# A few subtractions and the last combination of an attention chunk move from GpSimd to VectorE, and the attention steps are placed anew

## The chip, the cores and the metric

The kernel runs on one core of a Trainium2 chip. The metric is the device time of one launch in microseconds. The engines are TensorE (PE in the rows, with its weight loads as PEld), VectorE (DVE), ScalarE (ACT), GpSimd (POOL) and the queue of SyncE (SP), which issues the transfers.

## The reference

Causal attention with a recalled memory term feeds a feed-forward layer with a squared ReLU, and that feeds four experts whose outputs are weighted per token.

```python
# q, k, v: (2, 8, 576, 64); M_prev: (2, 8, 64, 64); z_prev: (2, 8, 64)
a = softmax(where(causal, -1e9, q @ k.T / sqrt(64)))          # per batch and head
q_p = where(q > 0, q, exp(q) - 1) + 1
mem = (q_p @ M_prev) / (q_p . z_prev + 1e-6)
g = 1 / (1 + exp(-beta))                                      # per head
x = g * mem + (1 - g) * (a @ v)                               # -> 1152 tokens x 512

h = maximum(x @ w_in, 0) ** 2                                 # w_in: 512 x 2048
x = h @ w_out                                                 # w_out: 2048 x 512

p = domain_probs / (domain_probs.sum(-1) + 1e-9)              # 1152 x 4
out = sum_e p[:, e] * (maximum(x @ w1[e], 0) @ w2[e])         # w1: 4 x 512 x 1024
```

All inputs are float32.

## The kernel before

The 1152 tokens are nine tiles of 128, cut into three chunks that are worked in this order: tiles 7 and 8, tiles 0 to 3, tiles 4 to 6. While one chunk goes through the feed-forward layer, the attention of the next one is computed, so that TensorE has work of two kinds to alternate between. The change lies in the second of these stages: `ffn1(1, ...)`, the feed-forward layer of tiles 0 to 3 (512 tokens), runs beside `attention_b`, the attention of tiles 4 to 6. In the trace it lies between about 119.5 and 262 us.

Precision is kept by splitting each operand into a high and a low part and multiplying three of the four pairs (`PASS`). ScalarE makes the high part by a copy with rounding, another engine the low part by a subtraction. In the rows these are `w` (feed-forward weights, lines 83 and 84), `g` (hidden values, lines 793 and 794), `kst` (keys, lines 543 and 545), `qh` (queries, lines 549 and 550), `vct` (values, lines 566 and 568), `ah` and `al` (attention weights, lines 625 and 626) and `x` (the feed-forward layer's input, lines 205 and 206).

The feed-forward generator runs over 16 blocks f of 128 hidden columns. `up(f)` is 12 matmuls into one PSUM bank, `hpb` (line 106; `hpc` is the same in the stage after), which ScalarE (787) and VectorE (788) turn into `r`. That bank has one buffer, so the next `hpb` waits until `r` on VectorE has read it (the block f = 1 has a bank of its own). `down(f)` is 12 matmuls into the accumulators `y` (804). The generator yields after every three matmuls, 16 x 4 + 16 x 4 times, and once at its start: 129 yields.

`attention_b` goes over four groups j of two heads and, within each, over the tiles 4, 5 and 6. Tile 6 holds the last 64 tokens of both batches. One unit is one tile and one head group: score matmuls `sc` (589), masked maximum on VectorE (189), exponential on ScalarE (617), the split into `ah` and `al`, two transposing transfers on SyncE into `aht` and `alt` (630), and three units later the `pv` matmuls (656), which ScalarE copies to `xl` (661). The `pm` matmuls (669) give the memory term `xm`. Each piece is a step of the generator, and there are 58 of them. Beside the steps, `load(j)` brings in and splits the keys, queries and values of the next head group. The keys are stacked twice over the partitions, and the low part is written into the upper 64 partitions, in two halves for each of two batches: for batch 0 by GpSimd, for batch 1 by VectorE (545).

After the last unit of a tile, `combine` weighs the two terms: five small VectorE operations on `cf` (215 to 219), then `xm` times its weight (220), `xl` times its weight into `to` (223) and the sum (224). Then TensorE transposes `to` into `tp` (197), and ScalarE and VectorE copy that to `x`. The engines for 223 and 224 are arguments of `combine`. 220 is always on GpSimd.

`mix` sets how the two generators alternate: at each yield of the feed-forward layer it adds a ratio to a number that starts below zero, and runs one attention step for each whole one reached.

TensorE's order is the program's order. On the other engines the order is set by a scheduler ahead of time, and each engine runs its queue strictly in that order.

Of the kernel before, what the change touches and what calls it, by code (L numbers as in the profile page):

```python
# [10 lines left out]
F32 = mybir.dt.float32  # L11
# [11 lines left out]
B, H, S, D = 2, 8, 576, 64  # L23
# [21 lines left out]
def spread(a, b, lag=0.0):  # L45

    n = len(a) + len(b)
    keyed = [((i + 0.5) / len(a), 0, x) for i, x in enumerate(a)] + [(lag + (1 - lag) * (i + 0.5) / len(b), 1, x) for i, x in enumerate(b)]
    return [x for _, _, x in sorted(keyed, key=lambda k: k[:2])] if n else []
# [3 lines left out]
def attention_then_experts(ctx, tc, qa, ka, va, qc, kc, vc, mz, beta, w1, probs, w2, out):  # L53
# [11 lines left out]
    nc = tc.nc  # L65
# [47 lines left out]
    def run(g):  # L113
        for _ in g:
            pass

    def mix(main, side, ratio, due=0.0):

        for _ in main:
            due += ratio  # L120
            while due >= 1.0:
                due -= 1.0
                next(side, None)
        run(side)
# [16 lines left out]
    gp = kvs.enter_context(tc.tile_pool(name="gp", bufs=2))  # L141
# [5 lines left out]
    gate1 = kv.tile([P, H], F32, name="gate1")  # L147
# [20 lines left out]
    gate1v = kv.tile([P, H], F32, name="gate1v")  # L168
# [39 lines left out]
    def combine(t, pool, xl, xm, sm, guard, ps, muls, eng, nm=1, gate1=gate1, to=None):  # L208


        cf = pool.tile([P, 2, H], F32, tag="cf", name="cf", bufs=2)
        to = xl if to is None else to

        def zeroth():
            nc.vector.tensor_scalar_add(cf[:, 0], sm, guard)
            nc.vector.tensor_scalar_add(cf[:, 1], xm[:, :, D], 1e-6)
            nc.vector.reciprocal(out=cf, in_=cf)
            nc.vector.tensor_mul(cf[:, 0], cf[:, 0], gate1)
            nc.vector.tensor_mul(cf[:, 1], cf[:, 1], gate)
            nc.gpsimd.tensor_mul(xm[:, :, 0:D], xm[:, :, 0:D], cf[:, 1, :, None].to_broadcast([P, H, D]))  # L220

        def first():
            muls.tensor_mul(to, xl, cf[:, 0, :, None].to_broadcast([P, H, D]))
            eng.tensor_add(to, to, xm[:, :, 0:D])

        return [zeroth, first, lambda: finish(t, to, ps, nm)]
# [294 lines left out]
    def attention_b(pool, ps):  # L521
# [10 lines left out]
        def load(j):  # L532
            kraw, vraw = [], []
            for b in range(B):
                kraw.append(pool.tile([P, 2, S], F32, tag="kraw", name="kraw", bufs=2))
                nc.sync.dma_start(out=kraw[b], in_=kc[b, j])
            qraw = pool.tile([P, 4, 2, P], F32, tag="qraw", name="qraw", bufs=2)
            nc.sync.dma_start(out=qraw, in_=qc[j])
            for _ in range(4):
                yield  # L540
            for b in range(B):
                k = kst[b, j] = pool.tile([P, 2, S], F32R, tag=f"kst{b}", name="kst", bufs=2)
                nc.scalar.activation(out=k, in_=kraw[b], func=AF.Copy)
                for js in (slice(0, 1), slice(1, 2)):
                    (nc.vector if b else nc.gpsimd).tensor_sub(k[64:128, js], kraw[b][64:128, js], k[64:128, js].bitcast(F32))
                yield
                if b == 0:
                    qh = pool.tile([P, 2, 4, 2, P], F32R, tag="qh", name="qh", bufs=2)
                    tc.keep_in_program_order(nc.scalar.activation(out=qh[:, 0], in_=qraw, func=AF.Copy))
                    nc.vector.tensor_sub(qh[:, 1], qraw, qh[:, 0].bitcast(F32))  # L550
                    qst[j] = [qh]
                    yield
            e = pool.tile([P, 4, 2, P], F32, tag="phi", name="phi")
            nc.scalar.activation(out=e, in_=qraw, func=AF.Relu, scale=-1.0)
            nc.scalar.activation(out=e, in_=e, func=AF.Exp, scale=-1.0)
            nc.vector.scalar_tensor_tensor(out=qraw, in0=qraw, scalar=1.0, in1=e, op0=ALU.add, op1=ALU.max)
            qst[j].append(qraw)
            for b in range(B):
                vraw.append(pool.tile([P, 5, 2, D], F32, tag="vraw", name="vraw", bufs=2))
                nc.sync.dma_start(out=vraw[b].rearrange("p k j d -> p k (j d)"), in_=vc[b, j])  # L560
            yield
            for b in range(B):
                vt = vct[b, j] = pool.tile([P, 2, 5, 2, D + 1], F16, tag=f"vct{b}", name="vct", bufs=2)
                for p in range(2):
                    nc.gpsimd.memset(vt[:, p, :, :, D], 1.0 - p)
                nc.scalar.activation(out=vt[:, 0, :, :, 0:D], in_=vraw[b], func=AF.Copy, scale=vs)
                yield
                nc.vector.scalar_tensor_tensor(
                    out=vt[:, 1, :, :, 0:D], in0=vraw[b], scalar=vs, in1=vt[:, 0, :, :, 0:D], op0=ALU.mult, op1=ALU.subtract
                )  # L570
                yield
# [68 lines left out]
        def values(t, j):  # L640

            xl, xm, mx, nb = st[t]
            hs = slice(2 * j, 2 * j + 2)

            def pv_():
                ath, atl = at.pop((t, j))
                pv = ps.tile([P, 2, D + 1], F32, tag="m", name="pv")
                c = 0
                for b, r0, n in TILES[t]:
                    nk = -(-(r0 + n) // P)  # L650
                    qs = slice(c, c + n)
                    for jj in range(2):
                        todo = [(k, a, p) for k in range(nk) for a, p in ((ath, 0), (ath, 1), (atl, 0))]
                        for i, (k, a, p) in enumerate(todo):
                            kr = min(P, r0 + n - k * P)
                            nc.tensor.matmul(  # L656
                                pv[qs, jj, :], lhsT=a[0:kr, jj, k, qs], rhs=vct[b, j][0:kr, p, k, jj, :],
                                start=(i == 0), stop=(i == len(todo) - 1),
                            )
                    c += n  # L660
                nc.scalar.activation(out=xl[:, hs, :], in_=pv, func=AF.Copy)

            def mem():
                e = qst[j][1]
                pm = ps.tile([P, 2, D + 1], F32, tag="m", name="pm")
                for jj in range(2):
                    c = 0
                    for i, (b, r0, n) in enumerate(TILES[t]):
                        nc.tensor.matmul(
                            pm[c:c + n, jj, :], lhsT=e[0:64, t - LAST + i, jj, c:c + n], rhs=mzt[:, b, 2 * j + jj, :],  # L670
                            start=True, stop=True,
                        )
                        c += n
                nc.scalar.activation(out=xm[:, hs, :], in_=pm, func=AF.Copy)

            return pv_, mem

        units = [(t, j) for j in range(4) for t in tiles]
        lag = 3
        late = {}  # L680
        run(load(0))
        ahead = iter(())
        for i in range(len(units) + lag + 3):
            a, m = [], []
            if i < len(units):
                t, j = units[i]
                if t == tiles[0]:
                    run(ahead)
                    ahead = load(j + 1) if j < 3 else iter(())
                a = scores(t, j)  # L690
                m = [values(t, j)[1]]
            m = late.pop(i, []) + m
            if 0 <= i - lag < len(units):
                t, j = units[i - lag]
                m = [values(t, j)[0]] + m
                if j == 3:
                    xl, xm, mx, nb = st[t]
                    to = pool.tile([P, H, D], F32, tag="to", name="to")
                    fs = combine(
                        t, pool, xl[:, :, 0:D], xm, xl[:, :, D], 1e-9 * 2.0**14, ps, nc.gpsimd, nc.gpsimd, gate1=gate1v, to=to  # L700
                    )
                    m = m + [lambda fs=fs: (fs[0](), fs[1]())]
                    late[i + 1] = [lambda fs=fs: fs[2]()()]
            if a or m:
                for f in spread(a, m) if a and m else a + m:
                    f()
                    next(ahead, None)
                    yield
# [160 lines left out]
    with ExitStack() as cb:  # L869
        bp = cb.enter_context(tc.tile_pool(name="bp", bufs=1))  # L870
        with tc.tile_pool(name="ps_2", bufs=1, space=PSUM) as ps_2:
            mix(ffn1(1, ps_2, gp, 1), attention_b(bp, ps_2), 0.54, -11.0)
    kvs.close()


# [348 lines left out]
```

## Time and profile before

| what | us |
|---|---|
| median of three runs (698.75 to 699.38) | 699.31 |
| the profiled execution | 696.58 |
| its span, first to last instruction | 694.8 |
| TensorE busy in the span | 668.8 (96%) |
| VectorE busy | 516.2 (74%) |
| ScalarE busy | 450.0 (65%) |
| GpSimd busy | 159.7 (23%) |

The mean granted TensorE clock of the profiled execution is 0.998 of full speed, the higher of its two levels (2.4 GHz). Busy time of TensorE is the union of its matmuls, whose ends overlap in the pipeline, so a stretch without idle time can show 100%. The profiled execution is 2.7 us faster than the median of the runs, so differences are taken within its own time.

### The profile page before, as it was taken

How to read it: one execution, taken by the hardware profiler on the slowest of the kernel's cores; microseconds unless marked ns; L12 is line 12 of the kernel's file. 1: busy time of each engine (PE TensorE's matmuls, PEld its weight loads, DVE VectorE, ACT ScalarE, POOL GpSimd, SP SyncE). 2: the span in 40 equal slices, each digit the busy share in tenths (PEclk: the TensorE clock that was granted, in tenths of full speed). 3: DMA queues.
4: the chain of work that ended last, by engine and by line, in shares of the span. 5: the costliest groups of instructions: out<-in, count | busy, mean ns of one | idle time of the engine just before them, and what ended most of it. 6: DMA issues, size and time to landing. Idle time of an engine off the chain costs nothing.

```text
span 694.8 us, 12513 instructions
## 1 busy us (share of the span) xinstructions
PE 668.8 (96%) x4604; PEld 481.0 (69%) x4604; DVE 516.2 (74%) x1028; ACT 450.0 (65%) x862; POOL 159.7 (23%) x211
## 2 busy tenths in 40 slices
PE   7799999999999989999999999999999999999997
PEld 4688878776877869999666666666655555555553
DVE  7989786899786567589697579897765856665753
ACT  6789886888775549968777666555534535354440
POOL 1010010212200062003334424443332242423200
PEclk9999999999999999999999999999999999999999
DMA  9898884889585437864122432333331322000002
GB/s 302 259 386 298 273 277 143 291 234 236 163 162 118 101 93 246 302 191 149 62 90 92 122 104 79 122 118 125 123 121 62 94 90 91 30 1 1 2 1 75
DMA packets 65422, 101.25 MB, mean 146 GB/s; under 512 B 32656, under 2 KB 34704, under 8 KB 65360
## 3 DMA queue, kind: packets, MB, share of 16 engines
q1 hardware_dynamic: 65216, 100.45, 46.5%
q8 instruction: 36, 0.59, 0.3%
q14 instruction: 26, 0.21, 0.1%
q10 hardware_dynamic: 144, 0.00, 0.0%
HBM read 82.87 MB, written 10.75 MB: 135 GB/s over the span
## 4 chain that ended last, share of the span: by engine, by line
PE 65%; DVE 14%; DMA 7%; ACT 6%; issue 4%; POOL 2%; SPq 0%; DVEq 0%; ACTq 0%; POOLq 0%
PE o L1112 21%; PE pe L1015 18%; PE y L804 6%; DMA raw<-in_w 4%; PE y L802 4%; PE hpa L101 3%; PE hpb L106 3%; PE hpc L106 3%; PE pv L656 2%; DVE w L84 2%; PE pv L356 1%; PE sc L589 1%; DVE w L923 1%; PE sc L307 1%; DVE a L189 1%
## 5 line engine op out<-in xcount | busy, mean ns | idle before, releaser
L1112 PE MATMUL o<-w,g 128*128 128x512 f16 x864 | 217.5, 379 | 2.8 <-DVE g L1032 1.4
L1015 PE MATMUL pe<-xs,wu 128*128 128x256 f16 (+1 forms) x1344 | 196.3, 286 | 2.0 <-DVE u L1037 1.5
L1015 PEld LDWEIGHTS <-wu 128*128 128x128 f16 x1344 | 131.0, 98 | 70.3 <-issue 4.2
L1112 PEld LDWEIGHTS <-g 128*128 128x128 f16 x864 | 84.2, 98 | 72.0 <-DVE g L1032 2.6
L1031 ACT ACTIVATE g<-h 128x512 f16<-128x512 f32 (+1 forms) x64 | 43.3, 676 | 101.4 <-DVE h L1037 95.8
L804 PE MATMUL y<-g,w 128*128 128x512 f32 (+1 forms) x384 | 89.3, 369 | 0.0
L981 POOL TENSOR_TENSOR ws<-raw 128x256 f32<-128x256 f32 x32 | 24.3, 760 | 269.4 <-DVE wu L978 180.2
L804 PEld LDWEIGHTS y<-g,w 128*128 128x128 f32 x384 | 67.6, 188 | 7.2
L1032 DVE SCALAR_TENSOR_TENSOR g<-h,g 128x512 f16<-128x512 f32 (+1 forms) x64 | 51.4, 803 | 26.8 <-ACT g L1031 26.6
L1037 DVE SCALAR_TENSOR_TENSOR u<-pe,p 128x256 f32<-128x256 f32 (+1 forms) x64 | 29.0, 453 | 36.5 <-PE pe L1015 35.1
L84 DVE TENSOR_TENSOR w<-wraw,w 128x512 fp32r<-128x512 f32 x64 | 48.7, 769 | 8.8 <-ACT w L83 8.3
L106 PE MATMUL hpb<-x,w 128*128 128x512 f32 x192 | 51.1, 401 | 2.9 <-DVE r L788 2.9
L1037 DVE SCALAR_TENSOR_TENSOR h<-pe,u 128x256 f32<-128x256 f32 (+1 forms) x64 | 28.9, 454 | 30.3 <-PE pe L1015 30.1
L923 DVE SCALAR_TENSOR_TENSOR w<-raw,wpow,w 128x512 f16<-128x512 f32 x64 | 48.6, 763 | 0.0
L978 DVE SCALAR_TENSOR_TENSOR wu<-ws,wpow,wu 128x512 f16<-128x512 f32 x64 | 45.3, 747 | 2.4 <-ACT wu L989 2.3
L83 ACT ACTIVATE w<-wraw 128x512 fp32r<-128x512 f32 x64 | 39.6, 625 | 11.5 <-PE y L804 7.1
L189 DVE CUSTOM_DVE_ANT_0 a<-sc,mask 128x384 f32<-128x384 f32 (+4 forms) x80 | 36.6, 480 | 13.2 <-PE sc L589 10.6
L922 ACT ACTIVATE w<-raw,wpow 128x512 f16<-128x512 f32 x64 | 44.8, 709 | 0.5 <-PE o L1112 0.5
L919 ACT ACTIVATE junk<-raw 128x1024 bf16<-128x1024 f32 x32 | 33.7, 1052 | 16.2 <-DMA raw<-in_w 16.1
L106 PEld LDWEIGHTS hpb<-x,w 128*128 128x128 f32 x192 | 34.8, 188 | 11.2 <-DVE r L788 4.2
L983 ACT ACTIVATE wu<-raw,wpow 128x768 f16<-128x768 f32 x32 | 29.8, 931 | 14.1 <-PE pe L1015 10.9
L978 DVE SCALAR_TENSOR_TENSOR wu<-raw,wpow,wu 128x768 f16<-128x768 f32 x32 | 33.5, 1048 | 6.6 <-ACT wu L983 5.7
(173 smaller groups left out, 1115.6 us busy)
## 6 DMA issues: line engine op xcount, KB each, us to landing
raw<-in_w SPq DMA_DIRECT2D x64, 512.0 KB, 3.5
w<-in_w SPq DMA_DIRECT2D x32, 512.0 KB, 5.5
wraw<-w1s SPq DMA_DIRECT2D x64, 256.0 KB, 3.2
w1s<-bits SPq DMA_DIRECT2D x32, 256.0 KB, 4.1
kraw<-in_kc SPq DMA_DIRECT2D x8, 576.0 KB, 3.8
vraw<-in_vc SPq DMA_DIRECT2D x8, 320.0 KB, 4.2
qraw<-in_qc SPq DMA_DIRECT2D x4, 512.0 KB, 5.1
out<-acc SPq DMA_DIRECT2D x8, 256.0 KB, 2.1
```

The costliest lines, as they stand in the source:

```text
L84: eng.tensor_sub(w[:, 1], raw, w[:, 0].bitcast(F32))
L106: nc.tensor.matmul(acc, lhsT=w[:, a, kk * P:(kk + 1) * P], rhs=xs_r[c][:, b, kk, :], start=(i == 0), stop=(i == 3 * NK - 1),)
L189: nc.vector.tensor_tensor_reduce(out=dst, in0=sc, in1=msk, op0=ALU.add, op1=ALU.max, scale=1.0, scalar=-3.0e38, accum_out=m)
L804: nc.tensor.matmul(yacc[d], lhsT=w[:, a, d * P:(d + 1) * P], rhs=g[:, b], start=(first and i == 0), stop=(last and i == 2),)
L922: nc.scalar.activation(out=w0, in_=x, func=AF.Copy, scale=s)
L923: nc.vector.scalar_tensor_tensor(out=w1, in0=x, scalar=s, in1=w0, op0=ALU.mult, op1=ALU.subtract)
L978: nc.vector.scalar_tensor_tensor(out=w[:, 1, ks], in0=x, scalar=s1, in1=w[:, 0, ks], op0=ALU.mult, op1=ALU.subtract)
L1015: nc.tensor.matmul(acc, lhsT=w[:, wa, k, kk * P:kk * P + P], rhs=x[:, xb, kk], start=(m == 0 and not onto), stop=(m == 5), skip_group_chec ...
L1031: nc.scalar.activation(out=g[:, 0], in_=hm, func=AF.Relu)
L1032: nc.vector.scalar_tensor_tensor(out=g[:, 1], in0=hm, scalar=0.0, in1=g[:, 0], op0=ALU.max, op1=ALU.subtract)
L1037: nc.vector.scalar_tensor_tensor(out=out, in0=acc, scalar=HID, in1=x, op0=ALU.mult, op1=ALU.add)
L1112: nc.tensor.matmul(outs[t], lhsT=g[:, gb, r:r + P], rhs=w[:, wa], start=(p == 0 and m == 0 and k == 0), stop=(p == 3 and m == 1 and k == 2),)
```

## The change

Three lines differ. The low parts of batch 0's keys are made by VectorE as those of batch 1 already are. `combine` gets VectorE for the lines 223 and 224 in place of GpSimd. `mix` gets the ratio 0.556 in place of 0.54 and starts from -9.9 in place of -11.0.

```diff
--- before.py
+++ after.py
@@ -542,7 +542,7 @@
                 k = kst[b, j] = pool.tile([P, 2, S], F32R, tag=f"kst{b}", name="kst", bufs=2)
                 nc.scalar.activation(out=k, in_=kraw[b], func=AF.Copy)
                 for js in (slice(0, 1), slice(1, 2)):
-                    (nc.vector if b else nc.gpsimd).tensor_sub(k[64:128, js], kraw[b][64:128, js], k[64:128, js].bitcast(F32))
+                    nc.vector.tensor_sub(k[64:128, js], kraw[b][64:128, js], k[64:128, js].bitcast(F32))
                 yield
                 if b == 0:
                     qh = pool.tile([P, 2, 4, 2, P], F32R, tag="qh", name="qh", bufs=2)
@@ -697,7 +697,7 @@
                     xl, xm, mx, nb = st[t]
                     to = pool.tile([P, H, D], F32, tag="to", name="to")
                     fs = combine(
-                        t, pool, xl[:, :, 0:D], xm, xl[:, :, D], 1e-9 * 2.0**14, ps, nc.gpsimd, nc.gpsimd, gate1=gate1v, to=to
+                        t, pool, xl[:, :, 0:D], xm, xl[:, :, D], 1e-9 * 2.0**14, ps, nc.vector, nc.vector, gate1=gate1v, to=to
                     )
                     m = m + [lambda fs=fs: (fs[0](), fs[1]())]
                     late[i + 1] = [lambda fs=fs: fs[2]()()]
@@ -869,7 +869,7 @@
     with ExitStack() as cb:
         bp = cb.enter_context(tc.tile_pool(name="bp", bufs=1))
         with tc.tile_pool(name="ps_2", bufs=1, space=PSUM) as ps_2:
-            mix(ffn1(1, ps_2, gp, 1), attention_b(bp, ps_2), 0.54, -11.0)
+            mix(ffn1(1, ps_2, gp, 1), attention_b(bp, ps_2), 0.556, -9.9)
     kvs.close()
```

What the change moves on VectorE at the beginning of the stage is shown from the first `r` (line 788) to the third. `w_1609` and `w_1638` are two of the feed-forward layer's weight tiles. Before:

```order
L788 SCALAR_TENSOR_TENSOR r<-hpb,r 128x512
L84 TENSOR_TENSOR w_1609<-wraw,w_1609 128x512
L794 TENSOR_TENSOR g<-r,g 128x512
L545 TENSOR_TENSOR kst<-kraw,kst 64x576
L788 SCALAR_TENSOR_TENSOR r<-hpb,r 128x512
L84 TENSOR_TENSOR w_1638<-wraw,w_1638 128x512
L545 TENSOR_TENSOR kst<-kraw,kst 64x576
L794 TENSOR_TENSOR g<-r,g 128x512
L788 SCALAR_TENSOR_TENSOR r<-hpb,r 128x512
```

After:

```order
L788 SCALAR_TENSOR_TENSOR r<-hpb,r 128x512
L84 TENSOR_TENSOR w_1609<-wraw,w_1609 128x512
L545 TENSOR_TENSOR kst<-kraw,kst 64x576
L794 TENSOR_TENSOR g<-r,g 128x512
L545 TENSOR_TENSOR kst<-kraw,kst 64x576 x2
L788 SCALAR_TENSOR_TENSOR r<-hpb,r 128x512
L84 TENSOR_TENSOR w_1638<-wraw,w_1638 128x512
L550 TENSOR_TENSOR qh<-qraw,qh 128x1024
L794 TENSOR_TENSOR g<-r,g 128x512
L788 SCALAR_TENSOR_TENSOR r<-hpb,r 128x512
```

A third `kst` and `qh` now stand ahead of the third `r`, and the first `kst` ahead of the first `g`. The other operations are the same.

On TensorE the end of the stage moves. `tp` is the transposition of a combined tile, `y` the feed-forward layer's accumulators, `hpc` the first matmuls of the next stage. Before, from the last `pv` group on:

```order
L804 MATMUL y_1583<-g,w_3061 128x512 x3
L804 MATMUL y_1584<-g,w_3061 128x512 x3
L197 MATMUL tp<-ident,to 128x128 x4
L804 MATMUL y_1581<-g,w_3146 128x512 x3
L804 MATMUL y_1582<-g,w_3146 128x512 x3
L804 MATMUL y_1583<-g,w_3146 128x512 x3
L197 MATMUL tp<-ident,to 128x128 x4
L804 MATMUL y_1584<-g,w_3146 128x512 x3
L106 MATMUL hpc<-x_76,w_3295 128x384 x12
```

After, from the last `tp` on:

```order
L197 MATMUL tp<-ident,to 128x128 x4
L804 MATMUL y_1583<-g,w_3097 128x512 x3
L804 MATMUL y_1584<-g,w_3097 128x512 x3
L804 MATMUL y_1581<-g,w_3225 128x512 x3
L804 MATMUL y_1582<-g,w_3225 128x512 x3
L804 MATMUL y_1583<-g,w_3225 128x512 x3
L804 MATMUL y_1584<-g,w_3225 128x512 x3
L106 MATMUL hpc<-x_76,w_3295 128x384 x12
```

The last `tp` had three `y` matmuls between it and `hpc`, and now has 18. Between the last `pv` group and it there were 15 `y` matmuls and the `tp` of the tile before; now there are 12 and that `tp`.

On VectorE the combination of the first tile (`xl_1699`, `xm_1700`) stands, after the change, among these:

```order
L215 TENSOR_SCALAR cf<-xl_1699 128x8
L216 TENSOR_SCALAR cf<-xm_1704 128x8
L217 RECIPROCAL cf<-cf 128x16
L218 TENSOR_TENSOR cf<-cf,gate1v 128x8
L219 TENSOR_TENSOR cf<-cf,gate 128x8
L223 TENSOR_TENSOR to<-xl_1699,cf 128x512
L626 TENSOR_TENSOR al<-a,ah 128x2x576
L788 SCALAR_TENSOR_TENSOR r<-hpb,r 128x512
L224 TENSOR_TENSOR to<-to,xm_1700 128x512
L84 TENSOR_TENSOR w_3295<-wraw,w_3295 128x512
```

The last two operations of the combination (223 and 224) were on GpSimd. Between them now lie the low part `al` of a unit of tile 6 and an `r`, and 220, which 224 needs, is still on GpSimd.

## Rows read from the trace of the kernel before

**Rows 1.** Busy us by engine in three stretches: PE, PEld, DVE, ACT, POOL, clock, DMA, GB/s.

```profile
120.00:170.00 50.00, 46.62 (x254) 36.67 (x254) 44.68 (x73) 44.29 (x73) 11.71 (x14) 1.00 0.85 249
170.00:240.00 70.00, 69.90 (x563) 55.96 (x562) 50.95 (x103) 45.40 (x77) 4.09 (x10) 1.00 0.64 145
240.00:262.00 22.00, 19.29 (x178) 14.78 (x177) 13.35 (x30) 11.45 (x22) 11.47 (x9) 1.00 0.35 91
```

**Rows 2.** Waits of TensorE, 112 to 264 us: total, times, longest.

```profile
PE hpb L106 <- DVE r L788: 2.9, 3, 1.6
PE tp L197 <- POOL to L224: 2.4, 2, 1.6
```

**Rows 3.** Timeline of TensorE: start, us, operation, idle before and what ended it.

```profile
132.58 1.66 PE L106 MATMUL hpb<-x,w 128*128 128x512 f32 x6 [1.62 <-DVE r L788]
...
166.40 1.63 PE L106 MATMUL hpb<-x,w 128*128 128x512 f32 x6 [0.98 <-DVE r L788]
...
248.64 0.66 PE L197 MATMUL tp<-ident,to 128*128 128x128 f32 x4 [1.65 <-POOL to L224]
...
259.77 0.66 PE L197 MATMUL tp<-ident,to 128*128 128x128 f32 x4 [0.78 <-POOL to L224]
...
261.84 2.35 PE L106 MATMUL hpc<-x,w 128*128 128x384 f32 x12 [0.29 <-DVE x L206]
```

**Rows 4.** The chain of waits around the stage's end: start, us, what.

```profile
243.18 0.17 ACT xl L661
...
244.18 1.04 POOL to L223
...
249.30 2.76 PE y L804 x12
...
252.06 2.83 PE pv L656 x60
...
258.21 1.52 POOL to L224
```

**Rows 5.** Timeline of GpSimd: its pairs of key subtractions in the first stretch.

```profile
125.21 3.26 POOL L545 TENSOR_TENSOR kst<-kraw,kst 64x576 fp32r<-64x576 f32 x2 [4.67 <-ACT kst L543]
...
138.23 3.68 POOL L545 TENSOR_TENSOR kst<-kraw,kst 64x576 fp32r<-64x576 f32 x2 [9.76 <-ACT kst L543]
...
156.03 4.29 POOL L545 TENSOR_TENSOR kst<-kraw,kst 64x576 fp32r<-64x576 f32 x2 [14.12 <-ACT kst L543]
```

**Rows 6.** Timeline of VectorE, 123 to 158 us and one row at 244.

```profile
123.53 0.69 DVE L788 SCALAR_TENSOR_TENSOR r<-hpb,r 128x512 f32<-128x512 f32 x1 [3.61 <-ACT r L787]
...
125.63 1.55 DVE L794 TENSOR_TENSOR g<-r,g 128x512 fp32r<-128x512 f32 x1 [0.81 <-ACT g L793]
...
127.37 1.72 DVE L545 TENSOR_TENSOR kst<-kraw,kst 64x576 fp32r<-64x576 f32 x1 [0.18 <-ACT kst L543]
...
130.44 0.76 DVE L545 TENSOR_TENSOR kst<-kraw,kst 64x576 fp32r<-64x576 f32 x1
...
131.84 0.68 DVE L788 SCALAR_TENSOR_TENSOR r<-hpb,r 128x512 f32<-128x512 f32 x1
...
140.54 2.53 DVE L84 TENSOR_TENSOR w<-wraw,w 128x512 fp32r<-128x512 f32 x2
...
157.38 1.65 DVE L794 TENSOR_TENSOR g<-r,g 128x512 fp32r<-128x512 f32 x1
...
244.43 2.01 DVE L626 TENSOR_TENSOR al<-a,ah 128x1152 f16<-128x1152 f32 x1 [0.32 <-ACT ah L625]
```

**Rows 7.** VectorE's operations by form, 190 to 240 us: busy us, mean ns, idle before.

```profile
L84 DVE TENSOR_TENSOR w<-wraw,w 128x512 fp32r<-128x512 f32 x12 | 8.1, 684 | 0.0
...
L794 DVE TENSOR_TENSOR g<-r,g 128x512 fp32r<-128x512 f32 x6 | 4.1, 691 | 1.7 <-ACT g L793 1.3
...
L626 DVE TENSOR_TENSOR al<-a,ah 128x1152 f16<-128x1152 f32 x2 | 2.7, 1355 | 1.4 <-ACT ah L625 1.4
...
L550 DVE TENSOR_TENSOR qh<-qraw,qh 128x1024 fp32r<-128x1024 f32 x1 | 1.2, 1220 | 0.0
```

## The prediction

> **What bounds the kernel now.** I first cut the stage that holds the change (attention of the third chunk beside the first feed-forward layer of the second, 120 to 262 us) into three stretches of busy time by engine [rows 1]. TensorE is the bound: it is idle for 50.00 - 46.62 = 3.38 us in the first stretch, 0.10 us in the second and 22.00 - 19.29 = 2.71 us in the last. So 6.19 us is all that the change can win here without taking work off TensorE, and it takes none off. VectorE is the engine that stands close behind: 44.68 of 50 us busy at first, later 50.95 of 70.
>
> Next, the waits of TensorE over the stage [rows 2]: 2.9 us of them end with `r` on VectorE (line 788, which empties the PSUM bank of `hpb`), 2.4 us with `to` on GpSimd (line 224, the last combination). The timeline of TensorE puts them in place [rows 3]: 1.62 us before 132.58 and 0.98 us before 166.40 are for `r`, 1.65 us before 248.64 and 0.78 us before 259.77 are for `to`; the first `hpc` of the next layer waits 0.29 us for `x`. The chain of waits around the stage's end says what is in those two [rows 4]: from ScalarE's copy `xl` to the transposes `tp` run three GpSimd operations, one after the other. So the early wait is one for VectorE's queue, the late one for GpSimd's latency, and they need separate sums.
>
> **First part: the low key parts on VectorE.** Eight subtractions of 64x576 go from GpSimd to VectorE, two for each of four head groups. VectorE already does the eight for the other batch; such a one takes 0.76 us when nothing disturbs it (the one at 130.44, [rows 6]). Six of the moved eight fall in the first stretch: 6 x 0.76 = 4.56 us on an engine that has 50 - 44.68 = 5.32 us free there.
>
> Against that stands what GpSimd's copies cost VectorE now. GpSimd runs pairs of them from 125.21, 138.23 and 156.03 [rows 5]. Inside those pairs VectorE's operations with two SBUF inputs are long: `g` 1.55 and 1.65 us, one `kst` 1.72 us, two `w` together 2.53 us [rows 6], against 0.69 for `g`, 0.76 for `kst` and 2 x 0.68 less their overlap for `w` (8.1 us busy for 12, so 1.35 for two) [rows 6, 7]. The excess is 0.86 + 0.96 + 0.96 + 1.18 = 3.96 us in these rows alone. If it all goes, the move adds 4.56 - 3.96 = 0.6 us to VectorE; that is nearly level, and the two left over (the fourth head group, in the second stretch) add 1.52 us where 70 - 50.95 = 19 us are free, so I cost them at nothing and at 1.52 us if that cover is gone. If none of the excess goes, the first stretch pays up to 4.56 us.
>
> The Trainium skill ("SBUF — State Buffer", section "Who interferes with whom") says that a VectorE instruction with two SBUF inputs and a GpSimd instruction that reads SBUF exclude each other for the whole instruction. By that, all of the excess goes with the GpSimd copies, and the sum is the one with 0.6 us; the rows above agree, since 1.72 against 0.76 us is a wait and not a small slowing.
>
> How this meets TensorE can be counted at one place, the 1.62 us wait for the third `r`. Before, between the `r` at 123.53 and the one at 131.84 VectorE does two `w`, two `g`, one `r` and two `kst`, with 0.86 + 0.96 us of excess and 0.81 + 0.18 us idle [rows 6]. Now, by the order, it does a third `kst` and `qh` as well, 0.76 + 1.22 us [rows 6, 7]. With excess and idle time gone (the first `kst` needs only ScalarE's copy and fills the hole ahead of `g`) that is 1.98 - 1.82 - 0.99 = -0.83 us: the third `r` comes 0.8 us earlier, and half of the wait of 1.62 us is left.
>
> **Second part: denser and sooner.** The stage's main generator yields 129 times; attention has 58 steps. With 0.54 and -11 step n runs at the first yield k with 0.54 k - 11 >= n: the 23rd for the first, the 128th for the last. With 0.556 and -9.9 these are the 20th and the 123rd. At yield 50 attention has done 0.556 x 50 - 9.9 = 17.9 steps against 16.0, so 1.9 steps more. A step's VectorE work: of 44.68 + 50.95 = 95.6 us in the first two stretches some 39 belong to the feed-forward layer (14.5 rounds of four operations of about 0.68 us, [rows 1, 7]), which leaves 57 us for some 52 steps, 1.1 us each. So 2.1 us of VectorE work comes ahead of yield 50 that now comes behind it. Its price on TensorE lies between 0 (it fills the holes that the earlier start opens) and 2.1 us (the queue stays full and every `r` is later). What the steps issue moves with them: the loads of raw keys on SyncE, which wait for their buffer until the subtractions have read it, now wait for shorter ones, so the `wraw` loads queued behind them aren't held up longer; GpSimd's queue keeps only memsets and the three multiplications.
>
> For the first stretch I take 1.5 us won of 3.38: the 0.8 us counted, and of the other 1.8 us something under half, since excess that is gone (2.1 us of it after 131.84) and steps that come sooner (2.1 us) are level. The ends are 3.38 us won and 4.56 us lost. For the second stretch I take 0.
>
> **Third part: the last combination.** Two of its three operations per tile, the multiplication of `xl` (line 223) and the addition (224), go to VectorE; the one of `xm` (220) stays on GpSimd. That is a new wait: the addition waits for GpSimd, in VectorE's order with `w`, `g` and later `r` queued behind it.
>
> For the first tile, from the end of `xl` (243.35) to `tp` (248.64) are 5.29 us now. Between the `pv` group and `tp` TensorE has the same cover before and after (18 matmuls of `hpb` and `y`, and one `pv` group of 24). After the small operations on `cf` (to 244.18, 0.8 us, [rows 4]) VectorE now does the multiplication 0.69, `al` 1.36 to 2.01, the `r` of `hpb` 0.69 and the addition 0.69: 4.2 to 4.9 us in all, with the long `al` where it still meets GpSimd's `xm` [rows 6, 7]. So 0.4 to 1.1 us of 1.65 go, and what is left may be seen as a wait of `hpb` for that `r`, which stands behind the multiplication and `al`, instead of one of `tp`. The earlier steps also put six `hpb` matmuls ahead of that `pv` group where three `y` stood, which gives ScalarE about 0.7 us more (three matmuls of 2.76/12 us, [rows 4]) before `xl`. I take 0.5 us left, between 0 and 1.25.
>
> For the last tile, `pv` ends at 252.06 + 2.83 = 254.89 and `tp` starts at 259.77: 4.88 us. GpSimd's 1.04 for the multiplication goes beside `xm`, the addition falls from 1.52 [rows 4] to 0.69, and a subtraction of `x` (0.69) may stand between them: 3.0 to 3.7 us. The cover becomes 12 matmuls and `tp` of the tile before, 2.76 + 0.66 = 3.4 us [rows 3, 4]. I take 0.2 us left of 0.78. Behind that `tp` 18 `y` matmuls now stand instead of 3 before the next layer's first `hpc`: 4.1 us, against the 261.84 - 259.77 = 2.07 us that pass today from that `tp` over ScalarE's and VectorE's copies of `x` to the `hpc` that waits for them [rows 3], so its 0.29 us goes. In all 2.0 us won of 2.71, between 1.2 and 2.71.
>
> **Sum.** 1.5 + 0 + 2.0 = 3.5 us. The profiled execution took 696.58 us (span 694.8 and 1.78 around it), so 693.1 by it. The runs' median is 699.31, 2.7 us above the profiled one, which changes none of the differences: 699.31 - 3.5 = 695.8.
>
> **Rivals.** *Everything idle goes.* The port is what keeps VectorE late, and with it free `r` is never waited for: 3.38 + 2.71 = 6.1 us, 693.2. For it speaks that 0.10 us idle in the second stretch shows what this stage does when VectorE has room; against it, that the first stretch has VectorE work in front of `r` before and after.
>
> *The gain at the end is given back early.* The 1.9 steps cost their full 2.1 us as waits for `r`, the moved subtractions are level, and the end wins 2.0: 699.4, no change. For it speaks how little of VectorE is free there, 5.32 us in fifty; against it the 0.8 us counted at the first wait.
>
> *VectorE becomes the bound (slower).* The excess isn't given back because it comes from something other than GpSimd's copies, so six subtractions cost 4.56 us in front of the `r`s of the first stretch, the end wins 2.0: +2.6, 701.9. It decides from the point where VectorE's free 5.32 us there are used up, which 4.56 + 2.1 us would do. Against it stand the excesses, which lie only where GpSimd's copies lie.
>
> The Trainium skill ("Perfetto Trace Analysis", section "Optimizing Scalar/DVE Operations") says that with VectorE saturated it may make sense to move work to GpSimd, which speaks against this change and for the last rival; it adds that the two share a read port so that moving between them might not help. By the first half the time is 701.9, by the second that of the forecast.
>
> **Chances.** Forecast 0.62 (its own range 694.2 to 697.5), everything idle 0.11, given back 0.17, VectorE the bound 0.10. About 0.2% (1.4 us) is what a measurement can tell: faster 0.73, same 0.17, slower 0.10. The range takes in the first three cases: 693.4 to 699.4.
>
> **What would show it.** In the profile after: no VectorE `g`, `w` or `kst` above about 1 us between 120 and 170; TensorE's idle time there about 1.9 us, the first of it under 1 us and ended by `r`; none of its waits ended by GpSimd, `tp` waiting for the addition on VectorE or `hpb` for `r` for 0.7 us together in the last 22 us; the first `hpc` without a wait. The forecast is wrong if the waits for `r` in the first stretch grow beyond 2.9 us, or if the addition, waiting for `xm`, holds up VectorE so that `tp` stays where it is.

## The result and the profile after

| | before | after |
|---|---|---|
| median, us (6 runs each, taken in turn) | 699.26 (698.44 to 701.3) | 692.55 (692.16 to 694.88) |
| the profiled execution, us | 696.58 | 692.61 |
| its span, us | 694.8 | 690.6 |
| opening, to the first `hpb` of the stage | 119.5 | 122.2 |
| the stage, first `hpb` to first `hpc` | 141.6 | 136.9 |
| the next feed-forward layer, first `hpc` to first `pe` (line 1015) | 65.3 | 63.0 |
| the rest, to the end of the span | 368.3 | 368.5 |

The ratio is 0.9909, 95% interval 0.989 to 0.9929: 6.7 us faster. The prediction said 695.8 with a low end of 693.4, so it had the sign and missed the size by 3.2 us. The rows from "opening" on are read from the two traces. The opening took 2.7 us longer in the execution profiled after. The change touches nothing there, and in the fourteen profiles of this case the opening lies anywhere between 119.5 and 123.4 us, so executions are compared from the first `hpb` on: 575.3 us before, 568.4 after, which is 6.9 us and agrees with the medians. Two pieces make it: 4.7 us in the stage and 2.3 us in the layer that follows it, where the prediction had nothing; the rest is 0.2 us longer. (Some expectations below have 65.4 and 2.4 for that layer, from starts rounded to a tenth.)

First the windows of the kernel after that answer to [rows 1], cut by its own anchors (us, then busy time with instruction count of PE, PEld, DVE, ACT, POOL; granted clock, DMA share, GB/s). The last window is the next layer:

```profile
122.20:172.70 50.50, 49.05 (x267) 38.66 (x266) 45.13 (x81) 44.55 (x75) 0.47 (x8) 1.00 0.91 244
172.70:238.00 65.30, 65.30 (x546) 52.22 (x546) 49.53 (x107) 42.81 (x73) 0.76 (x8) 1.00 0.69 156
238.00:259.80 21.80, 21.39 (x189) 17.27 (x185) 15.35 (x33) 12.20 (x24) 4.36 (x3) 1.00 0.37 89
259.80:322.10 62.30, 62.30 (x362) 61.99 (x361) 49.60 (x93) 53.99 (x106) 7.75 (x8) 1.00 0.69 238
```

TensorE's idle time is 1.45, 0.00, 0.41 and 0.00 us. In stretches of before that are cut the same way it is 3.38, 0.10, 2.67 and 1.03. VectorE's busy time in the first stretch is 45.13 us, against 45.10 before: 81 operations instead of 74, six of the added ones subtractions, and level.

Next the waits of TensorE in the stage, which answer to [rows 2]:

```profile
PE hpb L106 <- DVE r L788: 1.2, 2, 0.8
PE pm L669 <- DVE qraw L556: 0.5, 1, 0.5
PE pm L669 <- ACT xl L661: 0.2, 1, 0.2
```

`to` is gone from the list; 2.9 us for `r` have become 1.2. The wait of `pm` for `qraw` is new. VectorE's timeline from the first `r` to the third answers to [rows 6] (start, duration, operation, idle time before it):

```profile
126.18 0.69 DVE L788 SCALAR_TENSOR_TENSOR r<-hpb,r 128x512 f32<-128x512 f32 x1 [3.57 <-ACT r L787]
...
127.76 0.76 DVE L545 TENSOR_TENSOR kst<-kraw,kst 64x576 fp32r<-64x576 f32 x1 [0.29 <-ACT kst L543]
128.54 0.69 DVE L794 TENSOR_TENSOR g<-r,g 128x512 fp32r<-128x512 f32 x1
129.27 1.43 DVE L545 TENSOR_TENSOR kst<-kraw,kst 64x576 fp32r<-64x576 f32 x2
...
133.67 0.69 DVE L788 SCALAR_TENSOR_TENSOR r<-hpb,r 128x512 f32<-128x512 f32 x1
```

`g` takes 0.69 us where it took 1.55, two `kst` 1.43 where one took 1.72. The third `r` starts 133.67 - 126.18 = 7.49 us after the first; before it was 131.84 - 123.53 = 8.31. On TensorE this is the first of these rows, which answer to [rows 3]:

```profile
134.41 2.34 PE L106 MATMUL hpb<-x,w 128*128 128x512 f32 x9 [0.80 <-DVE r L788]
...
243.52 0.97 PE L106 MATMUL hpb<-x,w 128*128 128x512 f32 x3 [0.41 <-DVE r L788]
244.35 0.66 PE L197 MATMUL tp<-ident,to 128*128 128x128 f32 x4
...
259.09 3.31 PE L106 MATMUL hpc<-x,w 128*128 128x384 f32 x18
262.24 0.28 PE L901 MATMUL yt<-ysq,ones 128*128 128x4 f32 x2
262.38 3.37 PE L106 MATMUL hpc<-x,w 128*128 128x384 f32 x18
```

The wait of 1.62 us is 0.80; at the end 0.41 us for `r` stands ahead of a `tp` that waits no more; the first `hpc` has no wait.

**Where the 2.3 us of the next layer lie.** The rows of the kernel before at the start and in the middle of that layer:

```profile
261.12 0.44 PE L106 MATMUL hpc<-x,w 128*128 128x384 f32 x1
...
265.04 3.37 PE L106 MATMUL hpc<-x,w 128*128 128x384 f32 x18
...
291.13 0.51 PE L106 MATMUL hpc<-x,w 128*128 128x384 f32 x2
292.17 2.00 PE L106 MATMUL hpc<-x,w 128*128 128x384 f32 x10 [0.53 <-DVE w L84]
294.01 2.24 PE L804 MATMUL y<-g,w 128*128 128x384 f32 x12
296.47 0.62 PE L106 MATMUL hpc<-x,w 128*128 128x384 f32 x2 [0.21 <-ACT w L83]
297.34 2.01 PE L106 MATMUL hpc<-x,w 128*128 128x384 f32 x10 [0.25 <-DVE w L84]
299.18 2.24 PE L804 MATMUL y<-g,w 128*128 128x384 f32 x12
```

A group of 12 matmuls comes every 2.08 us elsewhere in this layer (rows of 2.24, starts 2.08 apart). Here one takes 294.01 - 291.13 = 2.88 us and the other, due at 294.01 + 2.08 = 296.09, lasts to 299.18, which is 3.09. That is 0.80 + 1.01 = 1.81 us lost, with 0.99 idle. The first `hpc` group, with its wait of 0.29 us for `x` [rows 3], takes from 261.12 to the second at 265.04, 3.92 us, where the kernel after takes 262.38 - 259.09 = 3.29: 0.63 lost. Together 2.44 us; the kernel after loses 0.12 in a group of its own that takes 2.20 us (292.62 to 294.82), which leaves 2.3. A wait costs TensorE more than the idle time that the row shows.

### The profile page after: what moved, and what is told of

It is laid out like the page before. It is cut to its first block, busy times and chain, and to the rows that moved or that the text cites. A ratio compares the mean times of both kernels' runs of the same rounds, so it can differ in the third digit from the quotient of the medians.

```text
span 690.6 us, 12518 instructions
## 1 busy us (share of the span) xinstructions
PE 668.7 (97%) x4604; PEld 483.6 (70%) x4604; DVE 515.9 (75%) x1042; ACT 447.4 (65%) x862; POOL 137.6 (20%) x197
## 4 chain that ended last, share of the span: by engine, by line
PE 42%; DVE 5%; ACT 2%; DMA 2%; issue 1%; POOL 1%; DVEq 0%; ACTq 0%; SPq 0%; POOLq 0%
PE o L1112 22%; PE pe L1015 19%; DMA raw<-in_w 2%; DVE w L923 1%; DVE g L1032 1%; ACT g L1031 1%; DVE wu L978 1%; ACT wu L983 1%; DVE acc L1125 0%; DVE h L1037 0%; ACT wu L989 0%; PE y L804 0%; DVE u L1037 0%; ACT xs L922 0%; DVE w L84 0%
## 5 line engine op out<-in xcount | busy, mean ns | idle before, releaser
L1032 DVE SCALAR_TENSOR_TENSOR g<-h,g 128x512 f16<-128x512 f32 (+1 forms) x64 | 49.9, 780 | 26.5 <-ACT g L1031 26.4
L84 DVE TENSOR_TENSOR w<-wraw,w 128x512 fp32r<-128x512 f32 x64 | 45.3, 716 | 7.4 <-ACT w L83 7.4
```

The source lines that it names most:

```text
L84: eng.tensor_sub(w[:, 1], raw, w[:, 0].bitcast(F32))
L1032: nc.vector.scalar_tensor_tensor(out=g[:, 1], in0=hm, scalar=0.0, in1=g[:, 0], op0=ALU.max, op1=ALU.subtract)
```

## The experiments

Idle TensorE time in the stage's three stretches and the next layer, the length of both, and the median (of each kernel's own profile and runs; the ratio goes against runs of before taken in turn with it, whose median was 698.66 for e1 to e4, 699.69 for e5 to e8 and 699.50 for e9 to e12):

| kernel | idle, us | stage | next | median | ratio (95%) |
|---|---|---|---|---|---|
| before | 3.38 / 0.10 / 2.67 / 1.03 | 141.6 | 65.3 | 699.3 | |
| after | 1.45 / 0.00 / 0.41 / 0.00 | 136.9 | 63.0 | 692.55 | 0.9909 (0.989 to 0.9929) |
| e1 keys alone | 0.80 / 0.15 / 2.64 / 1.17 | 138.8 | 65.5 | 696.10 | 0.9965 (0.9947 to 0.9984) |
| e2 combination alone | 3.67 / 0.10 / 1.65 / 0.07 | 141.1 | 63.5 | 696.74 | 0.9976 (0.9956 to 0.9995) |
| e3 placement alone | 4.06 / 0.67 / 0.93 / 0.00 | 144.4 | 62.9 | 698.34 | 0.9995 (0.9972 to 1.0017) |
| e4 combination, placement | 5.23 / 0.67 / 0.41 / 0.03 | 143.4 | 63.2 | 697.25 | 0.9982 (0.9963 to 1.0001) |
| e5 keys, placement | 1.25 / 0.00 / 0.93 / 0.00 | 137.3 | 63.1 | 693.34 | 0.9912 (0.9882 to 0.9942) |
| e6 keys, combination | 0.80 / 0.15 / 1.64 / 0.07 | 137.7 | 63.7 | 694.22 | 0.9925 (0.9895 to 0.9954) |

### One part alone

Each takes one of the three lines of the change and leaves the other two as before.

```diff
 e1: nc.vector.tensor_sub(k[64:128, js], ...)          # else as before
 e2: combine(..., ps, nc.vector, nc.vector, ...)       # else as before
 e3: mix(ffn1(1, ps_2, gp, 1), attention_b(bp, ps_2), 0.556, -9.9)   # else as before
```

**e1, the keys alone.**

> Of the change, only the eight key subtractions go to VectorE; combination and step placement are as before. Theory A (each part pays by itself, the subtractions through the port they share with GpSimd): about 2 us faster than before, 697.3, with TensorE idle in the first 50 us of the stage down from 3.4 to about 1.5 us and no VectorE operation of 128x512 above 1 us there; the waits for the combination at the stage's end stay at 2.4 us. Theory B (the placement of the steps does nearly all, the engine moves little): within 0.5 us of before, or slower by up to 2 us, since 6 x 0.76 us come onto a full VectorE.

Measured: 2.6 us faster. All of it lies in the first stretch, where the idle time falls by 2.58 us. Waits of TensorE in its stage:

```profile
PE tp L197 <- POOL to L224: 2.4, 2, 1.6
PE hpb L106 <- DVE r L788: 0.8, 1, 0.8
PE hpc L106 <- DVE x L206: 0.3, 1, 0.3
```

The end is as it was (2.4 us for `to`), and so is the next layer. So the first part is worth more by itself than the 1.5 us that the prediction gave to it and to the sooner steps together.

**e2, the combination alone.**

> Of the change, only the last combination's lines 223 and 224 go to VectorE. Theory A: 1 to 2 us faster (697.3 to 698.3), by shorter waits of the transposes at the stage's end, and the first stretch unchanged. Theory B: at most 0.5 us faster, since the last tile's combination still ends three y matmuls before the next layer.

Measured: 1.9 us faster by the medians, and the interval reaches nearly to 1. The end gains 1.02 us of idle time, of the 2.0 that the prediction gave to it with the placement's help, and `tp` still waits 1.3 us, now for the addition on VectorE. The next layer takes 63.5 us instead of 65.3: its waits for `w` are gone (0.07 us idle), the one for `x` is not.

**e3, the placement alone.**

> Of the change, only the step placement (0.556 and -9.9); GpSimd keeps subtractions and combination. Theory A: about 2 us faster (697.3): the wait of the next layer's first matmuls for x goes, the combination's waits fall by the later start of what needs it, and the first stretch is no better, since GpSimd still holds VectorE up. Theory B: 5 us faster or more (694 or less), with the stage after it shorter by the 2.4 us that the whole change won there.

Measured: no change. Its rows on TensorE in the first stretch, and then its windows around the second wait (columns as above):

```profile
135.90 2.35 PE L106 MATMUL hpb<-x,w 128*128 128x512 f32 x9 [1.63 <-DVE r L788]
162.96 0.96 PE L106 MATMUL hpb<-x,w 128*128 128x512 f32 x3 [2.34 <-DVE r L788]
```

```profile
160.00:163.00 3.00, 0.66 (x4) 0.22 (x2) 3.00 (x11) 0.66 (x1) 1.42 (x1) 1.00 0.52 106
163.00:165.00 2.00, 2.00 (x8) 1.50 (x8) 2.00 (x5) 2.00 (x4) 0.00 (x0) 0.86 0.90 353
165.00:171.00 6.00, 5.91 (x16) 4.39 (x15) 5.32 (x9) 4.52 (x9) 0.00 (x0) 0.50 1.10 199
171.00:173.00 2.00, 2.00 (x30) 1.59 (x29) 1.86 (x5) 2.00 (x4) 0.00 (x0) 0.93 1.16 298
```

The end gains 1.74 us of idle time and the next layer 2.5 us; the first two stretches give it back. There GpSimd's pairs are still under way when the sooner steps come. VectorE and GpSimd in front of the second wait:

```profile
154.84 0.11 DVE L623 MEMSET ah<- 128x64 uint32 x1 [1.53 <-DMA aht<-ah]
...
157.68 2.47 DVE L556 SCALAR_TENSOR_TENSOR qraw<-qraw,phi 128x1024 f32<-128x1024 f32 x1
```

```profile
157.26 4.16 POOL L545 TENSOR_TENSOR kst<-kraw,kst 64x576 fp32r<-64x576 f32 x2 [12.28 <-ACT kst L543]
```

`qraw`, 1.22 us elsewhere, takes 2.47 inside a pair, and VectorE has stood 1.53 us before that for a transposing transfer to read `ah`. `r` and with it `hpb` come 2.34 us late, and then the granted clock is 0.50 (the 1.2 GHz level) for six microseconds, which before never shows in this stage. The stage is 2.7 us longer although TensorE's idle time in it, up to the first `hpc`, is 0.2 us shorter (5.66 against 5.91), so about 3 us go another way, which the six microseconds at half the clock account for: an estimate from this one execution. It took 701.07 us, 2.7 above the median of the kernel's twelve, and its mean clock of 0.989 is the lowest of them, so it isn't shown that the clock falls as far in every execution.

### Two parts

Each undoes one line of the change.

```diff
 e4: (nc.vector if b else nc.gpsimd).tensor_sub(k[64:128, js], ...)   # else as after
 e5: combine(..., ps, nc.gpsimd, nc.gpsimd, ...)                      # else as after
 e6: mix(..., 0.54, -11.0)                                            # else as after
```

> The change without the key subtractions, which stay on GpSimd. Theory A: the end of the stage is as with the whole change, the first stretch as before or worse by up to 2 us, so about 2 us slower than the whole change: 694.5. Theory B: as the whole change, 692.5, within 0.5 us.

> The change without the move of the last combination, which stays on GpSimd. Theory A (port and placement work together: with GpSimd's subtractions gone the sooner steps cost no wait for r, and the sooner end clears the next stage): first stretch idle about 1.5 us as with the whole change, one wait of tp for GpSimd of about 0.9 us left, next stage 63 us long: 693 to 694. Theory B (the combination's move carries the end): end and next stage as before, 696.

> The change without the new step placement. Theory A: the gains of the two moves add up, 2.5 + 1.9: 694.3, first stretch idle 0.8 us, waits of tp 1.3 us, next stage about 63.6 us; the new placement is then worth another 1.5 to 2 us. Theory B (the placement is worth nothing, as it was alone): as the whole change, 692.5.

Without the keys (e4) 5 of the 6.7 us are gone: the wait for `r` that e3 shows is 3.04 us here, and a stretch at the 1.2 GHz level follows it too. Without the combination (e5) the time can't be told from the whole change. Without the placement (e6) 5.5 us are won against the runs of before beside it, where the change wins 6.7, with intervals that overlap. In e5 the `tp` of the first tile still waits for GpSimd, and that of the last tile no longer does:

```profile
PE tp L197 <- POOL to L224: 0.9, 1, 0.9
PE hpb L106 <- DVE r L788: 0.8, 1, 0.8
```

```profile
242.68 0.66 PE L197 MATMUL tp<-ident,to 128*128 128x128 f32 x4 [0.93 <-POOL to L224]
```

So the parts don't add. Placement alone is worth nothing, but beside the moved keys it is worth what e5 has over e1: stage 138.8 to 137.3, next layer 65.5 to 63.1, ratio 0.9965 to 0.9912. The combination's move adds half a microsecond of idle time to that (0.93 to 0.41).

### Is it GpSimd's reading, or the order of the instructions?

e7 is the whole change, but GpSimd also does the subtractions that it lost, into 64 rows of `kraw` that nothing reads afterwards; the order on VectorE and ScalarE is that of after, operation for operation, in both this run and e8. e8 has it write the same rows instead: a one-column copy to keep the place, and three memsets per half.

```diff
 e7:
+                    if b == 0:
+                        nc.gpsimd.tensor_sub(kraw[b][0:64, js], kraw[b][0:64, js], k[0:64, js].bitcast(F32))
 e8:
+                    if b == 0:
+                        nc.gpsimd.tensor_copy(kraw[b][0:64, js, 0:1], k[0:64, js, 0:1].bitcast(F32))
+                        for _ in range(3):
+                            nc.gpsimd.memset(kraw[b][0:64, js], 0.0)
```

> The whole change, and besides GpSimd does subtractions of the form and number that it lost (64x576, two SBUF inputs, after ScalarE's copy of batch 0's keys), into key rows that nobody reads any more, so that no other engine waits for them but the transfer that refills the buffer. The order of all other engines is that of the whole change. Port theory: VectorE's operations with two SBUF inputs are long again while GpSimd runs (1.5 to 2.5 us instead of 0.7 to 1.2), the waits for r come back, and 3 to 5 us of the gain go: 695.5 to 697.5. Rival (the subtractions were slow to wait for, nothing more): within 0.5 us of the whole change, 692.5.

> As the run with the added subtractions, but GpSimd writes zeros into the same rows, three times each, after a copy of one column: it writes as much and more, and reads almost nothing. If only reads meet VectorE at the port: VectorE's operations as long as with the whole change, and 692.5 within 0.5 us. If any GpSimd access does: VectorE long again, and 1 us or more lost.

Measured: e7 699.84 us, ratio 1.0002 (0.998 to 1.0024): the whole gain is gone. e8 693.41, ratio 0.9922 (0.9893 to 0.9951): it is kept, and its stage takes 136.7 us, where that of after takes 136.9 and that of e7 142.9. VectorE of e7 from its first `g`, and GpSimd beside it:

```profile
128.75 1.82 DVE L796 TENSOR_TENSOR g<-r,g 128x512 fp32r<-128x512 f32 x1
130.60 2.56 DVE L545 TENSOR_TENSOR kst<-kraw,kst 64x576 fp32r<-64x576 f32 x2
...
141.37 2.05 DVE L570 SCALAR_TENSOR_TENSOR vct<-vraw,vs,vct 128x640 f16<-128x640 f32 x1
...
161.78 1.35 DVE L614 TENSOR_SCALAR nb<-mx 128x2 f32<-128x2 f32 x1
```

```profile
128.01 3.85 POOL L547 TENSOR_TENSOR kraw<-kraw,kst 64x576 f32<-64x576 f32 x2 [4.58 <-ACT kst L543]
141.10 3.63 POOL L547 TENSOR_TENSOR kraw<-kraw,kst 64x576 f32<-64x576 f32 x2 [9.24 <-ACT kst L543]
159.31 3.79 POOL L547 TENSOR_TENSOR kraw<-kraw,kst 64x576 f32<-64x576 f32 x2 [14.58 <-DVE w L84]
```

The same `g` took 0.69 us in the kernel after, the same two `kst` 1.43: 1.13 us more each time. Together with the 0.80 us that the change leaves that is 3.06, and the wait for the third `r` is 3.05. What TensorE waits for in e7, and then in e8, where GpSimd writes for about as long:

```profile
PE hpb L106 <- DVE r L790: 5.1, 3, 3.0
```

```profile
136.87 3.30 PE L106 MATMUL hpb<-x,w 128*128 128x512 f32 x9 [3.05 <-DVE r L790]
```

```profile
128.77 3.18 POOL L549 MEMSET kraw<- 64x576 f32 x6
139.93 3.17 POOL L549 MEMSET kraw<- 64x576 f32 x6
```

```profile
PE hpb L106 <- DVE r L792: 1.2, 2, 0.8
PE pm L673 <- DVE qraw L560: 0.4, 1, 0.4
```

That 1.2 us of e8 is what the kernel after has, and beside the memsets its `g` and its two `kst` take 0.69 and 1.43 us. It is GpSimd's reading of SBUF beside VectorE's that costs, not its being busy and not its writing. The Trainium skill ("SBUF — State Buffer", section "Who interferes with whom") says the same of VectorE instructions with two SBUF inputs: they contend with a GpSimd instruction that reads SBUF, not with one that only writes it. The traces agree, by the 1.82 us of `g` in e7 and the 0.69 in e8.

### The next layer's squares

In before, ScalarE does two squares of raw weights (line 919, 1.06 us each) ahead of the `w` copies that `hpc` waits for in the middle of the next layer, and stands 0.79 us for the first one's raw weights to land:

```profile
287.18 1.06 ACT L919 ACTIVATE junk<-raw 128x1024 bf16<-128x1024 f32 x1 [0.79 <-DMA raw<-in_w]
...
290.22 1.13 ACT L83 ACTIVATE w<-wraw 128x512 fp32r<-128x512 f32 x2
```

e9 is before without expert 0's eight squares; a constant stands in their place.

```diff
+    nc.vector.memset(wsq[:, 0], 0.41)
...
+                if e == 0:
+                    return
```

> The kernel before, without the eight squares of the first expert's raw weights on ScalarE in the stage after the changed one (their sum, which only sets a power of two for scaling, is put there as a constant). The transfers keep their order. ScalarE theory of the 2.4 us that the stage after lost before the change: its weight copies stand behind squares that wait for raw weights to land; without them that stage falls from 65.4 to about 63 us and the whole by about 2.2 us: 697. Rival (the late last tile of attention makes that stage late): the stage stays above 65 us and the whole at 699.

Measured: 698.53 us, ratio 0.9988 (0.9973 to 1.0003), no change that can be told; the next layer takes 65.5 us, as before. The two waits at 292 and 296 us are gone, and a longer one stands a little later, for a `w` that ScalarE copies behind two squares of another expert. Its group, due at 298.02, lasts to 301.44, 3.42 us in place of 2.08:

```profile
298.86 2.74 PE L106 MATMUL hpc<-x,w 128*128 128x384 f32 x12 [0.68 <-ACT w L83]
```

So those squares are not the cause by themselves. The traces show which parts matter. ScalarE, VectorE and SyncE do this layer in one order in before and e1 (65.3 and 65.5 us), in a second in e2 and e6 (63.5 and 63.7), and in a third in all runs with the new placement (63.0 in after). So the keys don't change the order; the placement does, and so does the combination in the old placement. But the order isn't all: e8 has that of after and takes 64.4 us, since ScalarE stands 1.25 us for raw weights to land, where after doesn't wait, and `w` is late once:

```profile
289.73 1.06 ACT L923 ACTIVATE junk<-raw 128x1024 bf16<-128x1024 f32 x1 [1.25 <-DMA raw<-in_w]
```

```profile
293.52 2.73 PE L106 MATMUL hpc<-x,w 128*128 128x384 f32 x12 [0.81 <-ACT w L83]
```

Which feature of the order decides, and what makes those transfers land sooner or later, is left open.

### Can the change be bettered?

```diff
 e10: (nc.gpsimd if j == 3 and b == 0 else nc.vector).tensor_sub(...)   # else as after
 e11: muls.tensor_mul(xm[:, :, 0:D], ...)     # line 220 on VectorE too, else as after
 e12: mix(..., 0.56, -10.5)                   # else as after
```

> The whole change, except that the two key subtractions of the fourth head group go back to GpSimd; they run after 180 us, where VectorE has room. Port theory: VectorE's operations get long there by 0.7 us as in the kernel before, but nobody waits for it: within 0.5 us of the whole change, 692.5. Rival (any such GpSimd read costs what the six early ones do per piece, about 1 us each): 694.5.

> The whole change, and the multiplication of xm (line 220) goes to VectorE too, so that GpSimd does no arithmetic in the stage. TensorE's idle time at the stage's end is 0.41 us with the whole change, so at most that much can be won: 692.1 to 692.6. If VectorE's queue there becomes what the transposes wait for: 693 or more.

> The whole change with 0.56 and -10.5 in place of 0.556 and -9.9: the first attention step one yield later, the last at the same yield. The waits left in the first stretch (0.80 us for r, 0.46 us for qraw, 0.20 us for xl) are to fall, the second above all, since pm is asked for later: 692.0 to 692.6. If later steps crowd VectorE more: 693 or more.

| kernel | median | ratio (95%) | waits of TensorE, stage and next layer |
|---|---|---|---|
| e10 | 693.13 | 0.9907 (0.9887 to 0.9927) | `r` 2.1 us in 3, stage 137.9 us |
| e11 | 693.56 | 0.9915 (0.9895 to 0.9934) | `to` 1.4, `r` 0.8, `w` 0.3 |
| e12 | 693.88 | 0.992 (0.99 to 0.994) | `r` 2.6 us in 3, `w` 0.8 |

None can be told from the change, none is below it. e10 puts a pair back on GpSimd (3.35 us at 185.22) in the stretch where VectorE has room, and the trace shows 0.61 us idle there instead of 0.00. In e11 `xm` stands behind `al` and `r` in VectorE's queue, and `to` is 1.4 us late. So the trace speaks for leaving line 220 on GpSimd, though it has a price there too: in the kernel after, an `al` of 1.35 us takes 2.20 beside the first `xm` (240.66), ahead of the `r` that TensorE waits 0.41 us for. The times can't tell the two apart.

## Why the prediction was wrong, step by step

**The excess that goes with GpSimd's copies.** Right, and shown by e7 against e8. VectorE's busy time in the first stretch is level to 0.03 us, where the sum had 0.6 us more; the two stretches don't hold quite the same work, since the stage gets on faster after.

**The third `r`.** Right: 0.82 us earlier where 0.83 was counted, and 0.80 us left of a wait of 1.62.

**1.5 us of 3.38 in the first stretch.** The mechanism was right, the size small: 3.38 - 1.45 = 1.93 us. What failed is the price of the steps that come sooner. They were set against the freed excess as level (2.1 us each); e6 and after differ only in the steps, and there the idle time goes from 0.80 to 1.45, so they cost 0.65 us: the two waits of `pm`, 0.46 us for `qraw` and 0.20 for `xl`, that e6 doesn't have. That holds only once the keys are moved: with the pairs still on GpSimd the same steps cost 0.68 us of idle time in e3 (3.38 to 4.06), 0.57 in the second stretch, and a stretch at the lower clock.

**Nothing in the second stretch.** Right: 0.10 us idle before, 0.00 after.

**2.0 us of 2.71 at the end.** The size was right: 2.67 - 0.41 = 2.26 us in stretches cut alike. The cause was put mainly on the three operations' engines, with the placement as a help of 0.7 us to the first tile and of 0.29 us to `hpc`. The runs turn it round: placement with the operations still on GpSimd leaves 0.93 us (e3, e5), the operations moved in the old placement leave 1.65 (e2, e6).

**"6.19 us is all that the change can win here".** This step failed. It bounds the stage, and the sum then put nothing outside it. In the next layer 1.81 us go that two late `w` cost; the prediction uses no row of that layer behind its first `hpc`. That they go with the placement, or with the combination, is shown; why `w` is late in one order and not in another stays open. The wait of the first `hpc` was seen to go and counted at its 0.29 us, while it cost 0.63. And within the stage, up to that `hpc`, the time won is 4.7 us for 4.0 us of idle time (5.91 to 1.86), since a row's idle time is not all that a wait costs. Of the 3.5 us 3.2 were meant for that part. The gap between 3.5 and 6.9 us is then: 1.8 for `w`, 0.3 for `x` beyond what was counted, 0.8 for idle time won in the stage beyond the 3.2, 0.7 for what its waits cost beyond their idle time, less 0.1 for a group of the next layer that is slower after and 0.2 by which the rest is longer; that leaves the 3.4 us, but for rounding. Without the next layer's part the time would lie inside the range.

**The rivals.** "Everything idle goes" gives 693.2, the nearest figure (the range, which was to take this case in, begins above it, at 693.4), but for a reason that isn't the one here: 1.9 us of idle time are left in the stage. That the gain is given back early is what the placement does alone (e3, 698.34), not what it does with the keys moved. VectorE as the bound fell: the excess came from GpSimd. Of the advice that the prediction took from the Trainium skill ("Perfetto Trace Analysis", section "Optimizing Scalar/DVE Operations") the first half, that work moved from a full VectorE to GpSimd may pay, did not hold: e1 won 2.6 us by moving it the other way. The second half, that the two share a read port so that such a move might not help, agrees with e7.

## What to carry to other kernels

Where VectorE is the engine waited for, look for GpSimd operations that read SBUF beside it, and add up by how much VectorE's rows inside their spans exceed the same rows outside. That much of VectorE's time comes back when they are moved, even onto VectorE: here 3.96 us or more came back for 4.56 us of moved work, and with nothing else moved 2.6 us were won (e1). Try two changes of one stage together as well as alone: placing work sooner paid only after the contention was gone (0.3 us alone, within the noise; some 3.7 us beside the moved keys, e5 against e1). And when a stage changes, read the next one's waits too, and price a wait by how late the group ends, not by the idle time of its row.

## Not expected of the hardware

A wait costs more than its idle time: 0.53 us idle cost 0.80, 0.21 and 0.25 together 1.01, 0.29 cost 0.63.

The contention shows on an operation on 128x2 numbers too: `nb`, 0.16 us elsewhere, took 1.35 while GpSimd subtracted (e7, 161.78).

After a wait of 2.34 us in e3, with TensorE busy 0.66 of three microseconds, the granted clock went to 0.50 for six microseconds; after the 3.05 us in e7 the windows of two microseconds from 137 on show 0.74, 0.50, 0.91. After waits of 1.62 us in before and 1.65 us in e7 it stayed at 1.00. So a late `r` can be paid twice.
